# Stage one of a long convolution: the last 128 columns of four tiles in one eviction of 1024, with two staging buffers and a new order

## The chip, the cores and the metric

The kernel runs on one core of one Trainium2 chip. The metric is the device time of one execution in microseconds (us); lower is better. The engines are TensorE (PE in the profile), VectorE (DVE), ScalarE (ACT), GpSimd (POOL) and SyncE (SP), which issues nearly all DMA transfers.

## The reference

There are 2048 tokens of 640 channels. Two branches start from the same normalised input and are multiplied at the end.

```python
xn = _layernorm(A_q)
# branch A: short filter, then a convolution as long as the sequence, per channel
k_shift = sum_t k_pad[:, t:t+S, :] * shift_k[:, ks-1-t]      # ks = 4 taps
kv = k_shift * v
y  = irfft(rfft(kv padded to 2S) * rfft(ssm_k padded to 2S))[:S]   # causal convolution
s  = xn * (y + kv * ssm_D)
# branch B: a feed-forward block, 640 -> 1728 -> 640
g  = silu(gelu(xn @ w1 + b1) @ w2 + b2)
out = A_q + s * g
```

## The kernel before

**The convolution by matmuls.** The long convolution is a transform over time in two factors, a product by channel, and the way back. `K` stands for the filter `ssm_k`, `U` for the data `kv`; each is 16 tiles of 128 partitions by 640 channels. Stage one (`K1_i`, `U1_i`, L340) multiplies the two halves of 64 partitions of tile `i` by a matrix of sines `W`. Each half gives 640 columns. The first 512 go into one half of a PSUM buffer of two banks (`ps`), so one tile's two halves fill a buffer, and one eviction of 1024 columns (`Ke_i`, `Ue_i`, L175) copies it as bf16 into a staging buffer `st`. The other 128 columns are the remainder: `K1r_r`, `U1r_r` (L351) do it for a pair of tiles, four matmuls into half of a two-bank buffer, and `Ker_r`, `Uer_r` copy those 512 columns to the same staging buffer. Then `Ks_r`, `Us_r` (L358) store the staging buffer, four rows of 640 by 128 partitions, to a scratch in HBM (`scrK`, `scrU`). There are four staging buffers and three two-bank PSUM buffers.

Stage two loads the scratches back in another order (`KL`, L516, `UL`, L517), multiplies by small matrices (`K2`, `U2` L528, remainder `X2` L542), and evicts in place (`Kf`, `Uf`, `Xf`). The products by channel (`pm`, `pq`, L557, DVE) use the staging buffers again, stage three (`j1`, `j1r`, L563) and its evictions (`je`, `jer`) follow, `cs` (L613) and `cl` (L622) go through a third scratch `scrC`, and `i2` (L630) is the last step back; `ym` and `ad` (L634, L638) combine it with branch B.

**Branch B.** `bn`, `rs`, `xn` (L372, L385, L391) are the layer norm of a tile, `xt` (L401) and `xe` its transpose and the copy out. `f1` (L421) with `ge` (Gelu on ACT, L427) is the first product; tokens go in four chunks of four tiles. Chunk 0 goes through `f1` in halves of 256 tokens, two groups of hidden units to a bank; the other chunks take 512 tokens at once. `f2` (L457) with `si` (Silu, L461) and `gx` (L463) is the second product, a tile in two halves. `f1`, `f2` and `xt` share two PSUM buffers of a single bank (`psf`).

**Other work at the front.** `warm` (L656) is eleven matmuls on zeros ahead of everything, the `dm` operations (L663) are further dummies, `wq`, `wr`, `ws` make the matrix `W` in three pieces, `wm` and `we` (L320) spread the four short-filter taps over the partitions ("wx" in the text below), and `kv` (L485 to L494) is the short filter times `v`, in five groups on DVE, whose last operation (`kv_4`, L494) frees the U tiles of the group.

**What sets the order.** Each operation is declared with what it reads, writes and holds. The string `ORDER` lists all of them; the program is emitted in that order, and each engine and DMA queue runs its own operations in that order, waiting on semaphores. A suffix `/A` or `/D` says which of ACT and DVE makes an eviction. A buffer of a pool is taken at its first user in `ORDER` and is free again after its last.

```python
TB = (0, 4, 8, NT)     # W pieces by tile
NWARM = 11
IDLE = ((3, 1), (5, 1), (10, 1), (5, 0))     # dummies: how many, into which psf bank
```

Of the kernel before, what the change touches and what calls it, by code (L numbers as in the profile page):

```python
# [99 lines left out]
def h3_block(ctx: ExitStack, tc: tile.TileContext, x_d, k_d, v_d, sk_d, K_d, D_d, w1_d, b1_d, w2_d, out_d):  # L100
# [228 lines left out]
    def stage1(src, src_b, scr_, sb_, nm):  # L329
        for r in range(NG):  # L330
            o = Buf(pool=st)
            ob = [Buf() for _ in range(3)]
            pair = (2 * r, 2 * r + 1)
            for i in pair:
                pb = Buf(pool=ps)

                def s1(e, i=i, pb=pb):
                    for h in range(2):
                        hs = slice(64 * h, 64 * h + 64)
                        nc.tensor.matmul(out=pb.v[:, h, :], lhsT=W_t[hs, i, :], rhs=src[i][hs, 0:512], start=True, stop=True)  # L340

                op("%s1_%d" % (nm, i), "PE", s1, reads=[src_b[i], Wb[piece(TB, i)]], writes=[pb], hold=[o])
                op("%se_%d" % (nm, i), "ACT|DVE", lambda e, i=i, pb=pb, o=o: evict(
                    e, o.v[:, 2 * (i % 2):2 * (i % 2) + 2, 0:512], pb.v), reads=[pb], writes=[ob[i % 2]], hold=[o])
# [327 lines left out]
ORDER = """
c0 xl0 xl1 grid skl zz warm fix one1 wq1 Dl b1l Kl4 xl2 xl3 wq0 wr1 wr0 ws1 K1_6 bn1 wq2 ws0 Ke_6/A wm0 id we0/A bn0
K1r_3 dm0 K1_7 dm1 Ker_3/A b1c wr2 bn5 one0 Kl1 wm1 wm2 dm2 Ke_7/A ws2 rs0 xn1 xt1 xe1/A xn0 xt0 bn7 K1_5 dm3 xe0/A
bn4 bn6 we1/D Ke_5/A w1l2 w1l1 w1l0 f1_0_0_6 ge_0_0_7 Kl3 kl0 f1_0_0_4 K1_4 w1l3 Ks_3 ge_0_0_6 K1r_2 we2/A f1_0_0_2
ge_0_0_5 rs2 bn2 bn3 rs1 Kl2 ge_0_0_4 Ker_2/D f1_0_0_0 xn6 xn5 Ke_4/A ge_0_0_3 ge_0_0_2 K1r_6 ge_0_0_1 ge_0_0_0 xn7
xn4 K1_14 xt6 xe6/D K1_12 Ker_6/A xt7 xe7/D xn3 kv0_0 kv0_1m kv0_1a Ke_12/A xn2 xt5 kv0_2m kv0_2a kv0_3m kv0_3a kl1
vl0 kv0_4 kv1_0 xt4 K1r_7 xe5/A xe4/A K1_13 xt3 f1_1_0_4 xe3/A f1_1_0_7 kv1_1m kv1_1a Ke_13/A ge_1_0_4 Ker_7/A
ge_1_0_7 kv1_2m kv1_2a f1_1_0_11 Ke_14/A f1_1_0_1 ge_1_0_11 Ks_2 K1_15 K1_8 K1r_4 ge_1_0_1 xt2 Ker_4/A Kl0 xe2/A
Ke_15/A f1_1_0_0 f1_1_0_9 ge_1_0_0 ge_1_0_9 K1_9 f1_0_0_10 Ke_8/A f1_1_0_2 ge_0_0_10 Ks_7 ge_0_0_11 f1_0_2_12 K1_11  # L680
K1r_5 Ke_9/A Da ge_1_0_2 K1_10 ge_0_2_12 f1h_0 Ke_11/A geh_0 Ks_4 f1_1_0_12 Ke_10/A f1_1_0_6 ge_1_0_12 K1_2 kl2 K1_3
f1_1_0_8 vl1 Ker_5/A ge_1_0_6 Ke_3/A f1h_1 Ks_5 K1r_0 Ks_6 w2l1 K1_1 ge_1_0_8 geh_1 f1_1_0_3 w2l0 Ke_1/A ge_1_0_3
Ker_0/A f1_0_1_0 ge_0_1_1 kv1_3m kv1_3a kv1_4 xl5 ge_0_1_0 f1_1_0_10 f1_1_0_5 Ke_2/A ge_1_0_10 U1_1 U1r_0 ge_1_0_5
K1r_1 kv2_0 f1_0_1_6 f1_0_0_8 Uer_0/A Ue_1/A ge_0_1_7 ge_0_1_6 kv2_1m U1_0 U1r_2 kv2_1a ge_0_0_9 ge_0_0_8 Uer_2/A
f1_0_1_2 Ker_1/A ge_0_1_3 ge_0_1_2 kv2_2m Ks_1 sm0 kv2_2a sm1 Ue_0/A f1_0_1_4 vl2 ge_0_1_5 ge_0_1_4 kv2_3m f1_0_1_10
K1_0 ge_0_1_11 bn12 U1_4 U1_5 ge_0_1_10 bn15 Ue_5/A Ue_4/A f1_0_1_8 Us_2 kl3 ge_0_1_9 ge_0_1_8 f2_7_1 si_7_1 gx_7_1
bn13 ss f2_0_1 Ke_0/A si_0_1 gx_0_1 bn14 Ks_0 f2_3_1 si_3_1 kv2_3a U1r_3 Us_0 Uer_3/A U1_6 U1_7 Ue_7/A f2_6_0 Ue_6/A
gx_3_1 U1r_1 kv2_4 U1_3 si_6_0 U1_2 f2_5_0 sx f2_1_1 Uer_1/A kv3_1m Ue_3/A rs4 kv3_0 Ue_2/A vl3 U1_11 U1r_5 si_5_0
xn15 gx_5_0 kv3_1a xn14 kv3_2m gx_6_0 xn12 kv3_2a U1_10 kv3_3m xt14 si_1_1 gx_1_1 Ue_11/A xe14/A Ue_10/A Uer_5/A
f2_4_1 xt12 kv3_3a si_4_1 U1r_4 gx_4_1 U1_8 U1_9 f2_6_1 xe12/A Ue_9/A Uer_4/A si_6_1 Ue_8/A f2_2_0 Us_3 kv3_4 kv4_1m  # L690
kv4_0 xl4 gx_6_1 si_2_0 kv4_1a xt15 xe15/A Us_5 U1_12 U1_13 KL2 bn11 U1r_6 Uer_6/A kv4_2m bn9 kv4_2a kv4_3m Ue_12/A
# [63 lines left out]
```

## Time and profile before

| what | value |
|---|---|
| runs of the kernel | 185.24, 185.7, 188.32 us; median 185.7 |
| the profiled execution: its own time | 185.44 us |
| the profiled execution: span, first to last instruction | 183.4 us |
| PE busy | 176.8 us, 96% |
| DVE busy | 157.8 us, 86% |
| ACT busy | 142.3 us, 78% |
| DMA | 50.32 MB, mean 274 GB/s |
| granted PE clock | 1.00 |

Shares are of the span. A row of a timeline has the start, the duration, engine, line, operation, output and input, and in square brackets the idle time of the engine before it with what ended it. Rows that follow each other can overlap by a little, as the engines start the next instruction before the last has drained, so the distance between starts is the cost of one in a row. The ends of matmuls are modelled. `SPq` is the DMA queue of SP; a DMA's landing is counted from its issue.

### The profile page before, as it was taken

What the parts mean: (1) busy time and instruction counts of PE and PEld (TensorE: products, weight loads), DVE (VectorE), ACT (ScalarE), POOL (GpSimd) and SP (SyncE); (2) the same over time, 40 slices, a digit from 0 to 9 for tenths busy, and PEclk for the clock granted to TensorE, in tenths of its full rate; (3) what the DMA queues carried; (4) which work ended last, traced back from release to release, by engine and by line L of the source; (5) the groups of instructions that cost most, each with busy time, mean ns of one, the idle gap of its engine ahead of it and who ended that gap; (6) DMA issues with size and microseconds to landing.
All of it is one profiled execution on the core that took longest, in us unless ns stands there. A gap on an engine that the chain in (4) does not pass through costs nothing.

```text
span 183.4 us, 5038 instructions
## 1 busy us (share of the span) xinstructions
PE 176.8 (96%) x2111; PEld 103.0 (56%) x2111; DVE 157.8 (86%) x261; ACT 142.3 (78%) x217; POOL 16.4 (9%) x32
## 2 busy tenths in 40 slices
PE   7998899999999999999999999999999999999992
PEld 2366545444877566666653343434334688898781
DVE  7799699999999999997589997999999631599992
ACT  5699999999999969867689989999989831641021
POOL 4404003600001520002000000000000000000000
PEclk9999999999999999999999999999999999999999
DMA  5999996599987995997999497880161857998183
GB/s 133 405 396 289 396 423 270 164 376 405 390 291 270 332 358 193 346 383 276 307 389 391 127 265 241 274 274 15 45 244 54 331 194 240 358 377 276 45 313 116
DMA packets 24503, 50.32 MB, mean 274 GB/s; under 512 B 3807, under 2 KB 18465, under 8 KB 24226
## 3 DMA queue, kind: packets, MB, share of 16 engines
q1 hardware_dynamic: 24334, 50.01, 76.4%
q8 instruction: 16, 0.26, 0.6%
q10 hardware_dynamic: 148, 0.01, 0.1%
q14 instruction: 5, 0.04, 0.1%
HBM read 31.14 MB, written 18.35 MB: 270 GB/s over the span
## 4 chain that ended last, share of the span: by engine, by line
PE 89%; ACT 8%; DVE 1%; issue 1%; ACTq 0%; DVEq 0%
PE psf L457 34%; PE psf L421 30%; PE ps L563 6%; PE ps L528 4%; PE ps L340 4%; PE psf L656 3%; ACT st L175 3%; PE ps L630 2%; PE psf L401 2%; PE ps L542 1%; ACT hT L427 1%; ACT xnT L175 1%; PE psf L435 1%; PE ps L351 1%; ACT W L233 1%; ACT L427 1%
## 5 line engine op out<-in xcount | busy, mean ns | idle before, releaser
L457 PE MATMUL psf<-w,hT 128*64 128x320 bf16 (+6 forms) x672 | 64.5, 299 | 0.0
L421 PE MATMUL psf<-xnT,w 128*128 128x512 bf16 (+1 forms) x320 | 62.7, 340 | 1.4 <-ACT hT L427 1.2
L457 PEld LDWEIGHTS <-hT 128*64 128x64 bf16 (+3 forms) x672 | 46.9, 106 | 15.3 <-issue 2.9
L421 PEld LDWEIGHTS <-w 128*128 128x128 bf16 x320 | 28.9, 97 | 29.9 <-issue 11.5
L175 ACT CAST ku<-ps 128x1024 bf16<-128x1024 f32 (+1 forms) x43 | 39.5, 950 | 2.2 <-PE ps L563 1.1
L175 ACT CAST st<-ps 128x1024 bf16<-128x1024 f32 (+1 forms) x46 | 39.4, 898 | 1.6 <-PE ps L340 1.6
L427 ACT ACTIVATE hT<-psf,b1f 128x512 bf16<-128x512 f32 (+1 forms) x64 | 37.3, 633 | 1.1 <-PE psf L421 0.5
L461 ACT ACTIVATE sl<-psf 128x320 bf16<-128x320 f32 (+2 forms) x32 | 14.1, 440 | 30.6 <-PE psf L457 29.6
L175 DVE CAST ku<-ps 128x1024 bf16<-128x1024 f32 (+1 forms) x24 | 27.9, 1174 | 4.9 <-PE ps L528 2.3
L557 DVE TENSOR_TENSOR st<-ku 128x2048 bf16<-128x2048 bf16 (+1 forms) x32 | 24.7, 818 | 0.1
L463 DVE TENSOR_TENSOR xn<-xn,sl 128x320 bf16<-128x320 bf16 (+2 forms) x32 | 10.0, 316 | 10.0 <-ACT sl L461 9.9
L492 DVE TENSOR_TENSOR ku<-ku 128x2560 bf16<-128x2560 bf16 (+1 forms) x15 | 18.2, 1215 | 0.3
L489 DVE TENSOR_TENSOR ku<-ku 128x2560 bf16<-128x2560 bf16 (+1 forms) x15 | 18.3, 1217 | 0.2
L372 DVE BATCH_NORM_STATS2 stats<-x 128x6 f32<-128x320 bf16 x32 | 13.9, 475 | 0.9 <-DMA x<-in_x 0.9
L634 DVE TENSOR_TENSOR xn<-ps,xn 128x640 bf16<-128x640 f32 x16 | 12.7, 816 | 1.6 <-PE ps L630 1.6
L563 PE MATMUL ps<-st,I 32*64 32x512 bf16 (+1 forms) x384 | 11.1, 344 | 0.0
L528 PE MATMUL ps<-ku,F 64*32 64x512 bf16 x256 | 9.9, 379 | 0.0
L563 PEld LDWEIGHTS <-I 32*64 32x64 bf16 x384 | 4.9, 104 | 6.0 <-issue 4.1
L494 DVE TENSOR_TENSOR ku<-ku 128x2560 bf16<-128x2560 bf16 (+1 forms) x5 | 7.1, 1426 | 0.1
L401 PE MATMUL psf<-ident,xn 128*128 128x128 bf16 x80 | 6.9, 219 | 0.3 <-DVE xnT L175 0.3
L401 PEld LDWEIGHTS <-xn 128*128 128x128 bf16 x80 | 5.1, 97 | 3.2 <-issue 2.4
L391 DVE TENSOR_SCALAR xn<-x,mv,rstd 128x640 bf16<-128x640 bf16 x16 | 6.5, 437 | 0.0
(72 smaller groups left out, 125.3 us busy)
## 6 DMA issues: line engine op xcount, KB each, us to landing
scrK<-st SPq DMA_DIRECT2D x8, 640.0 KB, 4.8
scrU<-st SPq DMA_DIRECT2D x8, 640.0 KB, 6.0
ku<-scrK SPq DMA_DIRECT2D x8, 640.0 KB, 5.4
ku<-scrU SPq DMA_DIRECT2D x8, 640.0 KB, 6.6
scrC<-ku SPq DMA_DIRECT2D x8, 640.0 KB, 4.2
ku<-scrC SPq DMA_DIRECT2D x8, 640.0 KB, 5.5
ku<-in_v SPq DMA_DIRECT2D x4, 640.0 KB, 10.2
out<-x SPq DMA_DIRECT2D x15, 160.0 KB, 1.9
```

What stands on the lines that cost most here:

```text
L175: (nc.scalar.copy if e == "ACT" else nc.vector.tensor_copy)(out=out_, in_=in_)
L372: nc.vector.bn_stats(out=stats[:, i, h, :], in_=x_t[:, i, h * H:(h + 1) * H])
L401: nc.tensor.transpose(out=o[:, t, :], in_=xn_t[:, i, t * P:(t + 1) * P], identity=ident[:])
L421: nc.tensor.matmul(out=pb.v[:, u * n:u * n + n], lhsT=w1_t[:, ft, t, :], rhs=xnTb[c].v[:, a // P:(a + n) // P, t, :], start=(t == 0), stop ...
L427: op("ge_%d_%d_%d" % (c, r, ft), "ACT", lambda e, c=c, ft=ft, u=u, a=a, n=n, pb=pb: nc.scalar.activation(out=hTb[c].v[:, ft, a:a + n], in_ ...
L457: nc.tensor.matmul(out=pb.v[m:n, 0:hw], lhsT=hTb[c].v[0:M, ft, q * P + m:q * P + n], rhs=w2_t[0:M, ft, hs], start=(ft == 0), stop=(ft == F ...
L461: op("si_%d_%d" % (i, h), "ACT", lambda e, pb=pb, s_=s_, hw=hw: nc.scalar.activation(out=s_.v[:, 0:hw], in_=pb.v[:, 0:hw], func=ACT.Silu), ...
L489: op("kv%d_%dm" % (r, j), "DVE", lambda e, i=i, n=n, j=j, t=t, wb=wb: nc.vector.tensor_tensor(out=t.v[:, 0:n, :], in0=k_t[:, i + 3 - j:i + ...
L492: op("kv%d_%da" % (r, j), "DVE", lambda e, n=n, t=t, a=a: nc.vector.tensor_tensor(out=a.v[:, 0:n, :], in0=a.v[:, 0:n, :], in1=t.v[:, 0:n, ...
L528: nc.tensor.matmul(out=pb[ri].v[32 * j:32 * j + 32, a, :], lhsT=F2_t[64 * a:64 * a + 64, ri, :], rhs=B.v[64 * a:64 * a + 64, j, 0:512], st ...
L557: nc.vector.tensor_tensor(out=o, in0=u, in1=k, op=ALU.mult)
L563: nc.tensor.matmul(out=pb[j // 2].v[64 * a:64 * a + 64, j % 2, 0:n], lhsT=I1_t[32 * j:32 * j + 32, t, :], rhs=rhs(slice(32 * j, 32 * j + 3 ...
```

## The change

- The remainder of stage one is done for four tiles at a time: eight matmuls fill both banks of a PSUM buffer, and one eviction copies 1024 columns to two staging buffers, two tiles' remainders to each. So K and U have four remainder groups each instead of eight.
- The four staging buffers become parts of one tile `st`, so that one instruction can address two of them, whichever two and in whichever order.
- A staging buffer is stored when its two tiles and the shared remainder are evicted. A group of four tiles holds two staging buffers from its first matmul on.
- The order is new throughout, with the choice of ACT or DVE for each eviction, and the dummies are 10, 6 and 5 instead of 3, 5, 10 and 5. All merged evictions are on ACT.

```diff
-    st_t = [sb.tile([P, 4, D], BF16, name="st%d" % i)[:] for i in range(4)]
+    st_a = sb.tile([P, 16, D], BF16, name="st")
+    st_t = [st_a[:, 4 * i:4 * i + 4, :] for i in range(4)]
...
     def stage1(src, src_b, scr_, sb_, nm):
-        for r in range(NG):
-            o = Buf(pool=st)
-            ob = [Buf() for _ in range(3)]
-            pair = (2 * r, 2 * r + 1)
-            for i in pair:
-                pb = Buf(pool=ps)
+        for g in range(NG // 2):
+            o = [Buf(pool=st) for _ in range(2)]
+            ob = [[Buf() for _ in range(2)] for _ in range(2)]
+            rest = Buf()
+            quad = range(4 * g, 4 * g + 4)
+            for i in quad:
+                pb, oi = Buf(pool=ps), o[i % 4 // 2]
...
-            def s1r(e, pair=pair, pb=pb):
-                for i in pair:
+            def first(o):
+                return 0 if o[0].v.offset < o[1].v.offset else 1
+
+            def s1r(e, quad=quad, pb=pb, o=o, first=first):
+                for i in quad:
+                    n = P * (i % 4 ^ 2 * first(o))
                     for h in range(2):
                         hs = slice(64 * h, 64 * h + 64)
-                        nc.tensor.matmul(out=pb.v[:, h, P * (i % 2):P * (i % 2) + P], lhsT=W_t[hs, i, :], rhs=src[i][hs, 512:D],
+                        nc.tensor.matmul(out=pb.v[:, h, n:n + P], lhsT=W_t[hs, i, :], rhs=src[i][hs, 512:D],
                                          start=True, stop=True)
...
-            op("%ser_%d" % (nm, r), "ACT|DVE", lambda e, pb=pb, o=o: evict(
-                e, o.v[:, :, 512:D].rearrange("p (i h) c -> p h i c", h=2),
-                pb.v[:, :, 0:2 * P].rearrange("p h (i c) -> p h i c", i=2)), reads=[pb], writes=[ob[2]], hold=[o])
-            op("%ss_%d" % (nm, r), "SP", lambda e, r=r, o=o: nc.sync.dma_start(
-                out=by_q(scr_)[:, 4 * r:4 * r + 4, :], in_=o.v), reads=ob + [o], writes=[sb_[r]])
+            def er(e, pb=pb, o=o, first=first):
+                d0, d1 = (o[first(o) ^ k].v[:, :, 512:D] for k in range(2))
+                dst = bass.AP(tensor=d0.tensor, offset=d0.offset, ap=[d0.ap[0], [d1.offset - d0.offset, 2], [2 * D, 2], [D, 2], [1, P]])
+                evict(e, dst, pb.v.rearrange("p h (r i c) -> p r i h c", r=2, i=2))
...
+            for r in range(2):
+                op("%ss_%d" % (nm, 2 * g + r), "SP", lambda e, g=g, r=r, o=o: nc.sync.dma_start(
+                    out=by_q(scr_)[:, 8 * g + 4 * r:8 * g + 4 * r + 4, :], in_=o[r].v), reads=ob[r] + [rest, o[r]], writes=[sb_[2 * g + r]])
...
-IDLE = ((3, 1), (5, 1), (10, 1), (5, 0))
+IDLE = ((10, 1), (6, 1), (5, 0))
```

The two orders, PE's part only, up to the first `f2` and around the last U tiles:

```
before: warm K1_6 wm0 K1r_3 dm0 K1_7 dm1 wm1 wm2 dm2 xt1 xt0 K1_5 dm3 f1_0_0_6 f1_0_0_4 K1_4 K1r_2 f1_0_0_2 f1_0_0_0
        K1r_6 K1_14 xt6 K1_12 xt7 xt5 xt4 K1r_7 K1_13 xt3 f1_1_0_4 f1_1_0_7 ... U1_1 U1r_0 K1r_1 ... U1_0 U1r_2 ... U1_4 U1_5 f1_0_1_8 f2_7_1
        ... K2_2 f2_3_0 f2_2_1 U1_14 U1r_7 U1_15 f2_0_0
after:  warm K1_6 wm2 wm0 dm0 wm1 dm1 xt0 xt1 dm2 f1_0_0_6 f1_0_0_4 K1_7 K1r_1 K1_5 f1_0_0_0 f1_0_0_2
        K1_14 K1_4 xt4 xt7 K1_12 xt5 xt6 K1r_3 xt2 K1_15 f1_1_0_6 f1_1_0_1 ... f1_0_1_8 f2_7_1
        ... U1r_2 U1_10 f2_5_1 f2_6_1 U1_11 U1_12 U1_13 xt14 f2_2_1 K2_2 f2_2_0 U1_15 U1r_3 U1_14 xt15 f2_3_0
```

ACT's part up to the first 512-column `f1` of chunk 1:

```
before: ws1 ws0 Ke_6 we0 Ker_3 Ke_7 ws2 xe1 xe0 Ke_5 ge_0_0_7 ge_0_0_6 we2 ge_0_0_5 ge_0_0_4 Ke_4 ge_0_0_3 ge_0_0_2
        ge_0_0_1 ge_0_0_0 Ker_6 Ke_12 xe5 xe4
after:  ws1 ws2 we0 Ke_6 we1 xe0 xe1 ws0 ge_0_0_6 ge_0_0_7 ge_0_0_4 ge_0_0_5 Ker_1 Ke_5 ge_0_0_1 ge_0_0_0 ge_0_0_3
        ge_0_0_2 Ke_4 xe7 Ke_12 xe6
```

The loads and stores on SP are reordered with the rest: the first U store comes later, ahead of it all eight K stores, and the store of the U tiles 8 and 9 stands behind two loads of stage two.

More of the change, by code (lines that the diff above doesn't have):

```diff
@@ L340, in s1 @@
                         nc.tensor.matmul(out=pb.v[:, h, :], lhsT=W_t[hs, i, :], rhs=src[i][hs, 0:512], start=True, stop=True)
[L342 to L344 removed]
+                op("%s1_%d" % (nm, i), "PE", s1, reads=[src_b[i], Wb[piece(TB, i)]], writes=[pb], hold=[oi])
@@ L345, in stage1 @@
+                op("%se_%d" % (nm, i), "ACT|DVE", lambda e, i=i, pb=pb, oi=oi: evict(
+                    e, oi.v[:, 2 * (i % 2):2 * (i % 2) + 2, 0:512], pb.v), reads=[pb], writes=[ob[i % 4 // 2][i % 2]], hold=[oi])
             pb = Buf(pool=ps)
-            def s1r(e, pair=pair, pb=pb):
-                for i in pair:
+            def first(o):
[3 more added lines that the diff above has]
+                    n = P * (i % 4 ^ 2 * first(o))
@@ new lines, in stage1 @@
+            op("%s1r_%d" % (nm, g), "PE", s1r, reads=[src_b[i] for i in quad] + [Wb[w] for w in sorted({piece(TB, i) for i in quad})], writes=[pb], hold=o)
+            op("%ser_%d" % (nm, g), "ACT|DVE", er, reads=[pb], writes=[rest], hold=o)
+            for r in range(2):
+                op("%ss_%d" % (nm, 2 * g + r), "SP", lambda e, g=g, r=r, o=o: nc.sync.dma_start(
+                    out=by_q(scr_)[:, 8 * g + 4 * r:8 * g + 4 * r + 4, :], in_=o[r].v), reads=ob[r] + [rest, o[r]], writes=[sb_[2 * g + r]])
@@ L670 @@
 NWARM = 11
-IDLE = ((3, 1), (5, 1), (10, 1), (5, 0))
+IDLE = ((10, 1), (6, 1), (5, 0))
 ORDER = """
[L673 to L681, printed above, removed]
@@ L716 @@
+os_15_0 f2_15_1 si_15_1 gx_15_1 ad_15_1 os_15_1
 """
```

76 lines of the change are left out of this document (41 added, 35 removed).

## The prediction

> **What bounds the kernel now.** I read the page first, then the busy times of the engines in stretches, and then the timelines of the stretches where TensorE (PE) is not full.
>
> ```profile
> span 183.4 us, 5038 instructions
> ...
> PE 176.8 (96%) x2111; PEld 103.0 (56%) x2111; DVE 157.8 (86%) x261; ACT 142.3 (78%) x217; POOL 16.4 (9%) x32
> ...
> 0.00:6.08 6.08, 4.88 (x13) 1.56 (x13) 4.99 (x17) 3.14 (x5) 2.22 (x13) 1.00 0.63 196
> 6.08:22.34 16.26, 14.72 (x133) 9.48 (x134) 13.59 (x35) 15.19 (x25) 4.12 (x7) 1.00 0.99 368
> 22.34:43.15 20.81, 20.36 (x133) 9.72 (x133) 20.50 (x15) 20.69 (x33) 4.32 (x8) 1.00 0.83 320
> 43.15:157.80 114.65, 114.65 (x1510) 63.95 (x1511) 97.15 (x151) 95.41 (x142) 5.72 (x5) 1.00 0.76 266
> 157.80:180.00 22.20, 22.17 (x327) 18.33 (x322) 21.02 (x44) 7.52 (x13) 0.00 (x0) 1.00 0.74 261
> 180.00:183.40 3.40, 0.00 (x0) 0.00 (x0) 0.55 (x2) 0.36 (x1) 0.00 (x0) 1.00 0.20 65
> ```
>
> After the length, the columns of a stretch are busy us of PE, PEld, DVE, ACT, POOL, then the granted clock and DMA. From 43.15 to 157.80 us PE is busy for all of 114.65 us, and to 180.00 it misses 0.03. ACT, which the change relieves, is full only before that: 15.19 of 16.26 and 20.69 of 20.81 us. So an eviction saved after 43 us buys nothing by itself. The time changes only if PE reaches a given amount of work sooner in the first 43 us, or if the new order puts a hole into the full 137 us.
>
> **The change part by part: the eviction.** Sixteen evictions of 512 columns (eight each for K and U) become eight of 1024. The columns of a timeline row are start and duration; the cost of one in a row of work is the distance to the next start.
>
> ```profile
> 37.87 0.58 ACT L175 CAST st<-ps 128x512 bf16<-128x512 f32 x1
> 38.34 0.70 ACT L427 ACTIVATE hT<-psf,b1f 128x512 bf16<-128x512 f32 x1
> 38.92 1.02 ACT L175 CAST st<-ps 128x1024 bf16<-128x1024 f32 x1
> 39.81 0.72 ACT L427 ACTIVATE hT<-psf,b1f 128x512 bf16<-128x512 f32 x1
> ...
> L461 ACT ACTIVATE sl<-psf 128x320 bf16<-128x320 f32 x30 | 13.2, 440 | 27.1 <-PE psf L457 26.1 <-ACT ku L175 0.9
> ```
>
> A 512 costs 0.47 us (37.87 to 38.34), a 1024 costs 0.89 (38.92 to 39.81). Two against one is 0.94 against 0.89: 0.05 us saved, 0.4 us over eight. The trace has no eviction into two buffers in runs of 128; the bounds are 0.89, the nearest row of this size, and 0.94 if the runs cost as much as the two pieces did. I take 0.89, as the 512s went through runs of 128 already. Neither end matters to the time: in the U half ACT waits 26.1 us for PE (L461 row), and the K half is counted below. The matmuls stay the same, four times four becoming two times eight, so PE gains nothing, and two dummy matmuls fewer fall into the front's sum.
>
> **The order at the front.** The rest is the rewritten order. Its first half-conversion (f1, L421) comes before most of the K tiles now.
>
> ```profile
> 6.01 0.61 PE L340 MATMUL ps<-x,W 64*128 64x512 bf16 x2
> 6.55 0.72 PE L320 MATMUL ps<-hT,ones 1*128 1x512 bf16 x2
> ...
> 8.83 0.82 PE L320 MATMUL ps<-hT,ones 1*128 1x512 bf16 x3
> 9.58 1.26 PE L663 MATMUL psf<-hT 128*128 128x256 bf16 x10
> 10.68 0.72 PE L401 MATMUL psf<-ident,xn 128*128 128x128 bf16 x10
> 11.34 0.39 PE L340 MATMUL ps<-x,W 64*128 64x512 bf16 x2
> ...
> 12.65 2.34 PE L421 MATMUL psf<-xnT,w 128*128 128x256 bf16 x20
> ...
> 22.34 4.48 PE L421 MATMUL psf<-xnT,w 128*128 128x512 bf16 x20 [0.16 <-ACT xnT L175]
> ...
> 40.59 2.33 PE L421 MATMUL psf<-xnT,w 128*128 128x512 bf16 x15 [0.20 <-ACT hT L427]
> 43.15 2.46 PE L421 MATMUL psf<-xnT,w 128*128 128x512 bf16 x10 [0.23 <-ACT hT L427]
> ...
> 52.49 0.59 PE L340 MATMUL ps<-ku,W 64*128 64x512 bf16 x4
> ...
> 54.12 5.88 PE L457 MATMUL psf<-w,hT 128*128 128x320 bf16 x42
> ...
> 11.31 1.29 ACT L175 COPY xnT<-psf 128x640 bf16<-128x640 bf16 x2
> 12.46 1.06 ACT L175 CAST st<-ps 128x1024 bf16<-128x1024 f32 x1
> 13.99 1.28 ACT L427 ACT_TABLE_LOAD   x1 [0.47 <-PE psf L421]
> 15.28 0.84 ACT L427 ACTIVATE hT<-psf,b1f 128x256 bf16<-128x256 f32 x2
> 16.01 0.59 ACT L175 CAST ku<-ps 128x512 bf16<-128x512 f32 x1
> ...
> 3.54 2.76 SPq L288 DMA_DIRECT2D w<-in_w x3
> ...
> w<-in_w SPq DMA_DIRECT2D x1, 640.0 KB, 7.2
> ```
>
> After the warm-up PE now runs: one K tile 0.54 (6.01 to 6.55), three L320 matmuls 0.75 (8.83 to 9.58), ten dummies 1.10 (9.58 to 10.68), two L320 matmuls 0.50, six dummies 0.66, two transposed tiles 0.66 (10.68 to 11.34). From 6.01 that is 10.22. ACT follows: wx eviction from 7.30 to 8.19, K eviction to 9.08, wx eviction to 9.97, two xnT copies of 0.575 (11.31 to 12.46 for two) to 11.12. So f1 starts at about 11.2 instead of 12.65. Its weights are the seventh load on SP in both orders; they land at 3.54 + 7.2 = 10.7, in time.
>
> From there to the first 512-column f1 (22.34 before) both orders put the same work through PE, seven K tiles, four L351 groups' worth, seven transposed tiles and four f1 pairs, and ACT sets the pace. Before, ACT has eight Gelus of 0.365 (15.28 to 16.01 for two), two 1024s, two 512s and two copies after 15.28: 2.92 + 1.78 + 0.94 + 1.15 = 6.79, ending at 22.07. The trace has 22.34, so 0.27 are waits. After, the table load comes 1.34 after f1's start (12.65 to 13.99), at 12.54; Gelus start 1.29 later, at 13.83. The list has four 1024s: 2.92 + 3.56 + 1.15 = 7.63, with the same 0.27 of waits ends at 21.73. A lead of 1.45 us at f1 has shrunk to 0.6. A K eviction that stood ahead of the table load (Ke_5) and a remainder of 1024 in place of one of 512 (with a wx eviction the other way) cost 0.84 there.
>
> From 22 us to the first f2, ACT's list is lighter: four U tiles and two U remainders, which it used to evict before the first Silu, come later, so fourteen 1024s and seven 512s (15.8 us) become fourteen 1024s (12.5). PE then sets the pace, and of its two waits for Gelu (0.20 and 0.23) I let a quarter vanish. The lead is 0.7 us (0.6 and 0.1), bounds 0 and 1.45 + 0.43 = 1.9.
>
> **The order behind, and the waits it adds.** Each store of U (and K) now waits for the matmuls of four tiles, and the four hold two of four staging buffers. PE's last U tiles wait for the last kv product on DVE.
>
> ```profile
> 78.43 3.98 PE L457 MATMUL psf<-w,hT 128*128 128x320 bf16 x28
> 82.35 0.39 PE L340 MATMUL ps<-ku,W 64*128 64x512 bf16 x2
> ...
> 79.97 0.88 DVE L372 BATCH_NORM_STATS2 stats<-x 128x6 f32<-128x320 bf16 x2
> 80.88 0.21 DVE L373 BATCH_NORM_AGGREGATE mv<-stats 128x2 f32<-128x12 f32 x1
> 81.01 0.77 DVE L494 TENSOR_TENSOR ku<-ku 128x1280 bf16<-128x1280 bf16 x1
> 81.70 0.32 DVE L463 TENSOR_TENSOR xn<-xn,sl 128x320 bf16<-128x320 bf16 x1
> ...
> DMA to landing us min/median/max: 3.4/4.8/7.0
> ```
>
> That product is done at 81.70 and PE takes it at 82.35, 0.65 to spare. In the new order DVE has two statistics of 1.04 (79.97 to 81.01) and one L463 of about 0.3 less before it, 2.4 us; PE has one f2 half of 1.96 (3.92 for two, 78.43 to 82.35) and one transposed tile of 0.33 less, 2.3. DVE's chain starts behind PE's transposes, so both engines lead by about 0.7 and the 0.65 stays: no wait, price zero. If that cover goes, PE stands still for what is missing, and behind it nothing else can start.
>
> The last U quad needs the buffer of the tiles 8 and 9. Their merged eviction is the third behind its matmuls on ACT (0.89 + 0.58 + 0.89, so 2.4 us), and PE has four f2 halves (7.84), five U tiles of 0.3 (0.59 for two at 52.49) and a transposed tile before the next merged group, 9.7 us, and the matmuls of one K2 on top. That leaves about 7.5 us for the store, and the stores took 3.4 to 7.0 us between 55 and 100 us (the last row above). No wait, with 0.5 to spare at the worst. The waiting eviction would hold up the whole of ACT: two tile evictions, the Silus that free PE's two banks, then the last two stores and all eight U loads behind them on SP.
>
> Later, K and U evictions are dealt between ACT and DVE nearly as before, the six f2 halves that cover the way through scrC stay six, and the chain after the last matmul (3.40 us) is the same. I cost these at zero; the cover is the 114.65 us in which PE never waited.
>
> **The sum.** The profiled execution took 185.44 us, its span and 2.04 around it. 185.44 - 0.7 = 184.7 us. The median of the runs shown is 185.7, 0.26 above that execution.
>
> **The rivals.** *The lead is eaten by 43 us.* For it: ACT is 99% full there (20.69 of 20.81), there are only two single banks for f1, and a 1024 in place of a 512 makes the gap between two Gelus 0.42 longer. Against: the list is 3.3 us shorter. PE's waits grow by 0.7: 185.4 us, no change.
>
> *The staging buffers bind (slower than before).* Place: the merged eviction of the last U quad, at about 80 us. It decides once the store of tiles 8 and 9 needs over 7.5 us; at 10.5, half as long again as the longest, ACT stands for 3.0 us, and PE, with two banks to fill, for nearly as much: 184.7 + 3.0 = 187.7 us. Against: all stores of that stretch landed within 7.0.
>
> *PE's clock.* Between 17 and 21.7 us the new order leaves PE short K tiles and transposes with waits for ACT between them. In the first 5 us the eleven warm-up matmuls took 4.88 us, 0.444 each, against 4.48 / 20 = 0.224 at 22.34. If PE fell back to that rate for as long as the warm-up lasted, it would lose 4.88 / 2, 2.4 us: 187.1. Against: the granted clock is 1.00 in every stretch, and PE stays busy more than half of the time. The Trainium skill ("TensorE: Matmul & The Clock Gate", Part 1) has the clock halved after an idle window of some 3.4 us, and Part 4 says that transposes do not count as busy in the same way. By that rule the stretch could just trip it; in the trace the matmuls at 22.34, behind transposes and K tiles as well, run at 0.224.
>
> *The whole lead stays.* If the 1.45 at f1 holds and both Gelu waits go: 185.44 - 1.9 = 183.5.
>
> **How the numbers follow.** Forecast 0.45, lead eaten 0.22, staging 0.12, whole lead 0.10, clock 0.08, anything worse 0.03. The range runs from a little under the whole lead, 183.3, to the staging case, 187.7. The bound of 2%, about what a measurement of this kernel can tell from no change, is 3.7 us: under 182.0 nothing here reaches (0.03), over 189.4 only two of the bad cases together or an unseen hole (0.07).
>
> **What would show it.** In the profile after: the eight merged evictions at 0.89 to 0.94 us from start to start; the first L421 at 11.2 (not 12.65), the first 512-column one at 21.7, the first L457 near 52 (54.12 less 1.2 for the four U tiles that moved behind it, their remainders and the lead); PE full from there to the end; the last L494 before the U tile that needs it. I am wrong if PE waits for ACT more than 2 us between 22 and 52, if it shows any wait near 80 or 93 us, or if matmuls of 512 columns take over 0.4 us apart after 17 us.

## The result and the profile after

The changed kernel takes 184.53 us in the median (184.39 to 185.18), against 185.70 for the kernel before: a ratio of 0.996, interval 0.9943 to 0.9978. By the 2% bound that is no change, and by the interval a gain of some 0.7 us. The later rounds agree: there the kernel before took 185.20 to 185.29 us (medians of 9 to 29 runs). Forecast was 184.7. The profiled execution took 184.39, its span 182.6 us.

The page's head, and the busy times in the same stretches as before:

```profile
span 182.6 us, 5023 instructions
...
PE 175.6 (96%) x2109; PEld 104.0 (57%) x2109; DVE 157.8 (86%) x258; ACT 143.9 (79%) x212; POOL 16.4 (9%) x32
...
6.08:22.34 16.26, 14.57 (x134) 9.53 (x134) 15.55 (x38) 14.97 (x25) 5.39 (x13) 1.00 0.94 336
22.34:43.15 20.81, 20.72 (x133) 9.72 (x132) 20.38 (x33) 20.05 (x31) 4.87 (x3) 1.00 1.00 370
43.15:157.80 114.65, 114.65 (x1530) 64.50 (x1529) 96.05 (x131) 98.53 (x143) 2.80 (x3) 1.00 0.76 267
157.80:180.00 22.20, 21.25 (x310) 18.61 (x306) 20.63 (x46) 6.94 (x13) 0.00 (x0) 1.00 0.67 231
```

PE is again busy for all of 114.65 us in the middle, and the granted clock is 1.00 throughout. Between 22.34 and 43.15 ACT has come down from 20.69 to 20.05 us and PE has gone up from 20.36 to 20.72. In the last stretch PE shows less only because it is done sooner.

Where the time went is read from PE's timeline, at six places that every kernel here passes:

```profile
6.02 0.39 PE L342 MATMUL ps<-x,W 64*128 64x512 bf16 x2 [0.46 <-DMA x<-in_ssm_k]
...
11.30 2.41 PE L431 MATMUL psf<-xnT,w 128*128 128x256 bf16 x20
...
21.84 4.48 PE L431 MATMUL psf<-xnT,w 128*128 128x512 bf16 x20
...
51.49 3.97 PE L467 MATMUL psf<-w,hT 128*128 128x320 bf16 x28
...
93.85 1.24 PE L431 MATMUL psf<-xnT,w 128*128 128x512 bf16 x5
...
156.64 0.71 PE L640 MATMUL ps<-ku,G 128*64 128x512 bf16 x8
```

These are the first K tile, the first f1, the first f1 of 512 columns, the first f2, the first f1 of the third and fourth chunk, and the first i2 product. The differences of their starts give a table that all later readings use. The four U tiles and two U remainders that stood ahead of the first f2 in the kernel before are taken out of its third stage and put into the fourth, to compare like with like:

```profile
45.54 0.39 PE L340 MATMUL ps<-ku,W 64*128 64x512 bf16 x2
45.77 0.28 PE L351 MATMUL ps<-ku,W 64*128 64x128 bf16 x4
45.88 0.28 PE L351 MATMUL ps<-x,W 64*128 64x128 bf16 x4
...
48.38 0.39 PE L340 MATMUL ps<-ku,W 64*128 64x512 bf16 x2
48.60 0.28 PE L351 MATMUL ps<-ku,W 64*128 64x128 bf16 x4
48.81 3.52 PE L421 MATMUL psf<-xnT,w 128*128 128x256 bf16 x30
...
52.49 0.59 PE L340 MATMUL ps<-ku,W 64*128 64x512 bf16 x4
53.01 1.26 PE L421 MATMUL psf<-xnT,w 128*128 128x256 bf16 x10
```

From start to next start they take 0.34 + 0.43 + 0.52 = 1.29 us.

| us | before | after | lead gained | predicted |
|---|---|---|---|---|
| first K tile to first f1 | 6.64 | 5.28 | 1.36 | 1.45 |
| to first 512-column f1 | 9.69 | 10.54 | -0.85 | -0.84 |
| to first f2 (U work taken out) | 30.49 | 29.65 | 0.84 | 0.1 |
| to first f1 of chunks 3 and 4 (U work in) | 42.06 | 42.36 | -0.30 | 0 |
| to first i2 | 62.75 | 62.79 | -0.04 | 0 |
| to the end of the span | 25.76 | 25.96 | -0.20 | 0 |

The sum is 0.81, and the spans differ by 0.8. The forecast of 0.7 was right in sum, with one stage mis-sized by 0.7 and three losses of 0.54 missed; that the two nearly cancel is luck. The first row is also the least certain. It compares one execution of each kernel, and in the profiles below the same front took 6.42 us twice in the order of before, and 5.28 to 5.75 in the new one. So the lead made there is 0.7 to 1.4 us, and the 0.81 fits the spans of these two executions alone.

Ratios and intervals here and below leave out executions in a slower state (of the kernel before, the one at 188.32 us) and so are not quotients of the medians, and two profiles below, of fifteen dummies and of the last w1 piece early, were taken in that state (granted clock 0.79 between 6 and 22 us), so that only their stages that begin behind 25 us are read.

### The profile page after: what moved, and what is told of

Its sections match the earlier page's. It is cut to its first block, busy times and chain, and to the rows that moved or that the text cites. A ratio compares the mean times of both kernels' runs of the same rounds, so it can differ in the third digit from the quotient of the medians.

```text
span 182.6 us, 5023 instructions
## 1 busy us (share of the span) xinstructions
PE 175.6 (96%) x2109; PEld 104.0 (57%) x2109; DVE 157.8 (86%) x258; ACT 143.9 (79%) x212; POOL 16.4 (9%) x32
## 3 DMA queue, kind: packets, MB, share of 16 engines
HBM read 31.14 MB, written 18.35 MB: 271 GB/s over the span
## 4 chain that ended last, share of the span: by engine, by line
PE 72%; DVE 11%; ACT 11%; DMA 2%; issue 2%; SPq 0%; ACTq 0%
PE psf L431 27%; PE psf L467 25%; DVE xn L644 6%; PE ps L573 6%; PE ps L538 5%; ACT st L176 4%; PE ps L342 4%; ACT hT L437 3%; DVE x L648 3%; DMA x<-in_ssm_k 2%; PE psf L411 2%; DVE xn L473 1%; PE ps L552 1%; DVE x L656 1%; ACT ku L176 1%
## 5 line engine op out<-in xcount | busy, mean ns | idle before, releaser
L431 PE MATMUL psf<-xnT,w 128*128 128x512 bf16 (+1 forms) x320 | 61.9, 340 | 0.1
L467 PEld LDWEIGHTS <-hT 128*64 128x64 bf16 (+3 forms) x672 | 47.5, 106 | 14.8 <-issue 3.2
L176 ACT CAST st<-ps 128x1024 bf16<-128x1024 f32 x39 | 39.3, 1028 | 0.3 <-PE ps L342 0.2
L176 DVE CAST ku<-ps 128x1024 bf16<-128x1024 f32 (+1 forms) x25 | 28.7, 1153 | 4.8 <-PE ps L573 2.6
L567 DVE TENSOR_TENSOR st<-ku 128x512 bf16<-128x512 bf16 (+1 forms) x32 | 25.0, 815 | 0.6 <-PE ps L573 0.5
L499 DVE TENSOR_TENSOR ku<-ku 128x2560 bf16<-128x2560 bf16 (+1 forms) x15 | 19.1, 1275 | 0.2
L502 DVE TENSOR_TENSOR ku<-ku 128x2560 bf16<-128x2560 bf16 (+1 forms) x15 | 18.2, 1214 | 0.2
L573 PE MATMUL ps<-st,I 32*64 32x512 bf16 (+1 forms) x384 | 11.2, 344 | 0.0
L176 ACT COPY xnT<-psf 128x640 bf16<-128x640 bf16 x12 | 8.4, 724 | 0.0
L401 DVE TENSOR_SCALAR xn<-x,mv,rstd 128x640 bf16<-128x640 bf16 x16 | 7.5, 492 | 0.1
```

The costliest lines, as they stand in the source:

```text
L176: (nc.scalar.copy if e == "ACT" else nc.vector.tensor_copy)(out=out_, in_=in_)
L431: nc.tensor.matmul(out=pb.v[:, u * n:u * n + n], lhsT=w1_t[:, ft, t, :], rhs=xnTb[c].v[:, a // P:(a + n) // P, t, :], start=(t == 0), stop ...
L467: nc.tensor.matmul(out=pb.v[m:n, 0:hw], lhsT=hTb[c].v[0:M, ft, q * P + m:q * P + n], rhs=w2_t[0:M, ft, hs], start=(ft == 0), stop=(ft == F ...
L499: op("kv%d_%dm" % (r, j), "DVE", lambda e, i=i, n=n, j=j, t=t, wb=wb: nc.vector.tensor_tensor(out=t.v[:, 0:n, :], in0=k_t[:, i + 3 - j:i + ...
L502: op("kv%d_%da" % (r, j), "DVE", lambda e, n=n, t=t, a=a: nc.vector.tensor_tensor(out=a.v[:, 0:n, :], in0=a.v[:, 0:n, :], in1=t.v[:, 0:n, ...
L567: nc.vector.tensor_tensor(out=o, in0=u, in1=k, op=ALU.mult)
```

## The experiments

Ratios are against the kernel before on the same chip, with 95% intervals. The cuts from an order show the part of the engines that the text names.

### Two evictions instead of the merged one

```diff
-            op("%ser_%d" % (nm, g), "ACT|DVE", er, reads=[pb], writes=[rest], hold=o)
+            for k in range(2):
+                op("%ser_%d_%d" % (nm, g, k), "ACT|DVE", lambda e, k=k, er=er: er(e, k), reads=[pb], writes=[rests[k]], hold=o)
```

> The changed kernel with one thing taken back: each 1024-column remainder is evicted by two instructions of 512 columns, one behind the other on the same engine, instead of one. Matmuls, banks and order stay. Theory (the rewritten order carries the gain, the merged eviction is worth nothing): ScalarE does 8 x 0.05 = 0.4 us more, four of them before 52 us, and the time stays within 0.3 us of the changed kernel, 184.4 to 184.8 us. Rival (the merged eviction carries it): the gain of about 1 us goes, 185.4 to 185.7 us.

Measured: 184.71 us, 0.9972 (0.9959 to 0.9985), within the 184.4 to 184.8 of the theory. With the kernel before at 185.22 us in this round, the rival's loss of the whole gain would be a ratio of 1, which the interval leaves out. So the order carries at least most of the gain; the difference of 0.2 us to the changed kernel lies inside both intervals, and the times cannot say that it is nothing. In this profile the third stage is 0.47 longer than in the changed kernel (30.12), nearly all of it in one wait. It looks as if the split cost that, until one sees the same unit in a kernel whose evictions are merged (the one with the y sums first, below):

```profile
27.32 0.74 PE L446 MATMUL psf<-xnT,w 128*64 128x256 bf16 x10 [0.43 <-ACT hT L438]
```

```profile
27.27 0.74 PE L445 MATMUL psf<-xnT,w 128*64 128x256 bf16 x10 [0.37 <-DMA w<-in_w]
```

The first row is of the split kernel, the second of the merged one. The unit is the first 64-row half of f1, and it waits for the last piece of w1. In the changed kernel the load of that piece is issued at 18.25 and took 8.4 us (first row, and the last row of the view of that tile's DMA), so it landed at 26.65, and the unit started at 26.68. In the split kernel the same load, issued at 17.52, took 9.8 us and landed at 27.3, which is when the unit started there, though the wait names a Gelu:

```profile
18.25 0.52 SPq L289 DMA_DIRECT2D w<-in_w  x1
...
DMA to landing us min/median/max: 8.4/8.4/8.4
...
26.68 0.74 PE L445 MATMUL psf<-xnT,w 128*64 128x256 bf16 x10
```

That wait comes and goes from one execution to the next with the load, whatever the evictions are. After the first f2 the split kernel needs 42.33 us to the next mark, the merged ones 42.32 to 42.36: there the saved 0.05 us per eviction buys nothing, as predicted.

### The order of before from 93 us, and from 147 us

Both orders have done the same set of operations at the first X2 (93 us) and again at 147 us, so they can be joined there.

```diff
 # e2_front_new
-ORDER = new order
+ORDER = new order up to xt8 (93 us) + order of before from f1_3_0_0 on
 # e4_tail_old
-ORDER = new order
+ORDER = new order up to gx_11_0 (147 us) + order of before from cl_5 on
```

> The changed kernel's code, with its order up to the first X2 (about 93 us, where both orders have done the same operations) and the order of before from there. Theory (the lead is made before 93 us and the new order behind loses a little of it): the first chunk-3 f1 starts at 93.8 to 93.9 us as in the changed kernel, 1.04 us ahead of before, and all of it reaches the end, 184.2 to 184.4 us. Rival (the order behind 93 us adds to the gain): 184.8 to 185.5 us.

> The changed kernel's code, with its order up to about 147 us and the order of before for the tail (f2, i2 and the outputs of the last two chunks). Theory (the new tail order loses 0.2 us of the lead, since the last i2 products wait for VectorE): last Silu at about 179.0 us and 184.2 to 184.4 us. Rival (the tails are worth the same): 184.4 to 184.7 us, the time of the changed kernel. Second rival (the old tail was fitted to the old middle): over 184.8 us.

Measured: 184.17 us, 0.9949 (0.993 to 0.9967), with the rest old, and 183.96 us, 0.9938 (0.9919 to 0.9958), with the tail alone old. Both stages behind the cut say why: 62.75 and 62.79 us to the first i2 (the middles are worth the same), and 25.71 and 25.65 us from there to the end, against 25.96 in the changed kernel. So the gain is made before 93 us, and by the profiles the new tail gives back 0.25 to 0.3 of it; the intervals of the three times overlap. The first chunk-3 f1 came at 94.24 in the first of the two, not at 93.8 to 93.9 as expected: that execution needed 5.75 us from the first K tile to the first f1, where the changed kernel's profile shows 5.28. This front stage varies from 5.28 to 5.75 over seven profiles in which its code is the same or nearly so, and the end moves with it.

### The y sums first

```diff
-ad_10 gx_8_0 ym_9 ym_0 ym_8
+ad_10 ym_9 ym_0 gx_8_0 ym_8
```

> The changed kernel with one VectorE instruction moved in the tail: the Silu product of tile 8 (second half) goes behind the y sums of tiles 9 and 0 instead of ahead of them. Theory (the tail's loss of 0.2 to 0.3 us is this: VectorE stands 0.49 us for a Silu with finished i2 banks behind it, so the second i2 after it waits 0.27 us): the eight i2 matmuls that took 0.81 us at 162.63 take 0.54, first i2 to the end of the last f2 22.24 us instead of 22.51, and the time 0.2 to 0.3 us below the changed kernel, 184.1 to 184.3 us. Rival (the wait comes from elsewhere in the tail, VectorE being nearly full there): 22.5 us and no change.

Measured: 184.49 us, 0.9952 (0.9932 to 0.9973). The rows of the changed kernel, then of this one:

```profile
162.63 1.01 PE L640 MATMUL ps<-ku,G 128*64 128x512 bf16 x8
163.44 2.10 PE L467 MATMUL psf<-w,hT 128*64 128x320 bf16 x28
...
161.33 0.33 DVE L473 TENSOR_TENSOR xn<-xn,sl 128x320 bf16<-128x320 bf16 x1 [0.49 <-ACT sl L471]
161.57 3.74 DVE L644 TENSOR_TENSOR xn<-ps,xn 128x640 bf16<-128x640 f32 x5
```

```profile
163.31 0.71 PE L640 MATMUL ps<-ku,G 128*64 128x512 bf16 x8
163.86 2.07 PE L467 MATMUL psf<-w,hT 128*64 128x320 bf16 x28
```

The eight i2 matmuls took 0.81 us and take 0.55 now, and the tail 25.67 instead of 25.96. In the profile the theory holds: VectorE stood 0.49 us for a Silu, with finished i2 banks behind it, and PE paid for it a little later, in a wait too short for a bracket of its own. The time does not show it: 184.49 is outside the 184.1 to 184.3 of the theory, by the ratios it came down by about 0.15 us, and that is inside the intervals. The span of this profile, 183.0, also holds the w1 wait of 0.37.

### Fifteen and ten dummies instead of five

```diff
-IDLE = ((10, 1), (6, 1), (5, 0))
+IDLE = ((10, 1), (6, 1), (15, 0))   # and (10, 0) in the second kernel
```

> The changed kernel with ten more dummy matmuls (fifteen instead of five) just ahead of the first f1, which adds 1.1 us to TensorE there and computes nothing else. Theory of the prediction (ScalarE sets the pace between the first f1 and 22 us, and it starts when f1 does, so the early f1 counts in full): first f1 at 12.4 us, first 512-column f1 at about 22.9, and 185.4 to 185.7 us, the whole gain gone. Rival (the early f1 is worth little, because the lead is made between 22 and 52 us by the lighter list of ScalarE): first 512-column f1 below 22.3 us, and 184.4 to 184.8 us.

> The changed kernel with five more dummy matmuls (ten instead of five) just ahead of the first f1, half of the earlier step. Theory (the early f1 counts one for one): first f1 and first 512-column f1 0.45 to 0.55 us later relative to the first K tile than in the changed kernel, and the time 0.4 to 0.6 us longer, half-way between the changed kernel and the one with fifteen, about 185.0 us. Rival (what the front gives is fixed by data that arrive later, and only fifteen dummies cross that point): no change, 184.4 to 184.6 us.

Measured: 185.53 us, 1.0022 (1.0005 to 1.0038), with fifteen, and 184.99 us, 0.9984 (0.9967 to 1.0002), with ten. With the changed kernel at 0.996 that is 1.15 and 0.44 us for 1.1 and 0.55 us of dummies. The first is clear of both intervals, the second is not. With ten, first f1 stands 5.78 us behind the first K tile, which five dummies reached once too (5.75), and the next three stages are 10.54, 29.63 and 42.32: nothing there absorbs the delay. But these two profiles have one wait that no other profile here has behind 96 us, for a load of the third scratch in the tail. The row is of the kernel with ten dummies; with fifteen the same wait is 0.73 us:

```profile
166.66 0.73 PE L640 MATMUL ps<-ku,G 128*64 128x512 bf16 x8 [0.45 <-DMA ku<-scrC]
```

Their tails take 26.57 and 26.88 us in place of 25.96, so 0.6 and 0.9 more. So the medians fit an early f1 that counts one for one, but the profiles do not separate it from this load, and whether the dummies make the load late is not shown.

### The U work later in the kernel before

```diff
-f1_1_0_5 U1_1 U1r_0 K1r_1 ... U1_0 U1r_2 f1_0_1_2 ... K1_0 U1_4 U1_5 f1_0_1_8 f2_7_1 si_7_1 f2_0_1 si_0_1 f2_3_1 si_3_1
+f1_1_0_5 K1r_1 ... f1_0_1_2 ... K1_0 f1_0_1_8 f2_7_1 si_7_1 U1_1 U1r_0 f2_0_1 si_0_1 U1_0 U1_4 U1r_2 f2_3_1 si_3_1 U1_5
```

> The kernel before (single remainders, its own order) with one move: the four U tiles, the two U remainders and the store that stand before the first f2 go behind the first three f2 halves, with their evictions behind the first Silus, as the changed order has it. Theory (between 22 and 52 us TensorE was late for Gelu, because ScalarE also had these evictions; without them its waits go): first f2 at 54.12 - 1.29 (the moved TensorE work) - 0.6 to 0.85 = 52.0 to 52.2 us, waits for Gelu before it under 0.1 us, and the time 0.5 to 0.9 us below before. Rival (those waits come from the K tiles and the two single banks, the U evictions only fill ScalarE): first f2 at 52.6 to 52.9 us, and the time within 0.2 us of before.

Measured: 187.59 us, 1.0128 (1.0096 to 1.016). My theory fell. The third stage is 30.62, not shorter than the 30.49 of before without the U work, and the two waits for Gelu are where they were:

```profile
40.74 2.33 PE L421 MATMUL psf<-xnT,w 128*128 128x512 bf16 x15 [0.20 <-ACT hT L427]
43.30 2.46 PE L421 MATMUL psf<-xnT,w 128*128 128x512 bf16 x10 [0.23 <-ACT hT L427]
...
58.83 0.29 PE L351 MATMUL ps<-ku,W 64*128 64x128 bf16 x4 [0.67 <-ACT st L175]
...
62.72 0.39 PE L340 MATMUL ps<-ku,W 64*128 64x512 bf16 x2 [0.85 <-ACT st L175]
```

They stand ahead of the first U eviction (46.23 us in the kernel before), so taking those away cannot help. What the move did is in the last two rows: put between the first f2 halves in a bunch, the U evictions overrun ScalarE, and PE waits 1.52 us for banks; the stage takes 44.24 us instead of 42.06. The changed order spreads the same work and shows no such wait.

### One K tile and one K remainder later as well

```diff
-f1h_1 K1r_0 K1_1 f1_1_0_3 ... f1_0_1_6 f1_0_0_8
+f1h_1 f1_1_0_3 ... f1_0_1_6 K1r_0 K1_1 f1_0_0_8
```

> The kernel before with the U work moved behind the first f2 as in the run e7_u_later, and then one K tile and one K remainder (matmuls and evictions) moved from 40 us to the room at 46 to 50 us that this leaves. The stretch from the first 512-column f1 to the first f2 is what counts here, 30.62 us in e7_u_later, 29.65 in the changed kernel; the time itself carries the loss of e7_u_later behind 53 us and tells nothing. Theory (the 0.8 us gained there come from K evictions that no longer stand between Gelus bunched before 46 us; the U work only has to leave room for them): the waits of 0.20 and 0.23 us for Gelu go, and the stretch takes 29.9 to 30.2 us. Rival (the waits come from the order of the f1 units on their two banks): the stretch stays at 30.5 to 30.7 us with waits for Gelu of 0.3 us or more.

Measured: 187.96 us in a single run, and a third stage of 31.14 us, longer by 0.52 and outside both ranges:

```profile
40.36 4.50 PE L421 MATMUL psf<-xnT,w 128*128 128x512 bf16 x25 [0.65 <-ACT hT L427]
...
50.65 0.60 PE L421 MATMUL psf<-xnT,w 128*128 128x256 bf16 x4 [0.45 <-ACT hT L427]
```

The wait of 0.20 grew to 0.65, and the one of 0.23 behind it is gone. The first ends 18.24 us into the stage (40.36 less 22.12), as in the run before (40.74 less 22.49): the moved evictions stood behind the Gelu that it waits for, and the K tile was work that PE did while ScalarE freed one of the two single banks. The second was a wait for a Gelu behind the moved evictions. The rows are ScalarE's, in the kernel before and then in this one:

```profile
41.37 1.01 ACT L175 CAST st<-ps 128x1024 bf16<-128x1024 f32 x1
42.41 0.69 ACT L427 ACTIVATE hT<-psf,b1f 128x512 bf16<-128x512 f32 x1
```

```profile
41.64 0.69 ACT L427 ACTIVATE hT<-psf,b1f 128x512 bf16<-128x512 f32 x1 [0.51 <-PE psf L421]
```

Without the eviction ahead of it, this Gelu waits for PE. What lengthens the stage is the new wait of 0.45, behind the place to which the evictions were moved. So my theory held for one wait and the rival for the other: PE's waits go by which evictions stand just ahead of a Gelu on ScalarE, and by what PE has to do until it is done.

### The store that the last U quad waits for

```diff
 # e8_late_store
-U1_12 Us_4 U1_13 xt14 xe14 Us_2 ... KL3 gx_6_1 Us_5
+U1_12 U1_13 xt14 xe14 Us_2 ... KL3 gx_6_1 Us_5 Us_4
 # e8c_buffer_bound
+U1_12 U1_13 xt14 xe14 ... KL3 gx_6_1 Us_5 Us_4 Us_2
```

> The changed kernel with the store of U tiles 8 and 9 moved behind the store of tiles 10 and 11 on SyncE, about 3.2 us later (from 71.6 to about 75). Nothing else is moved. Theory (the staging buffers are what the last U quad waits for once that store is late; in the changed kernel it lands some 0.5 us before the merged eviction at 79.66): landing 7 to 8 us after issue, so ScalarE stands 2.5 to 3.5 us before the last merged U eviction, TensorE runs out of free banks about 1.5 us after that began and waits 1 to 3 us near 82 us, and the time is 185.5 to 187.5 us. Rival (a store issued later lands sooner, 5 us or less, because fewer transfers run beside it): no wait over 0.5 us and 184.4 to 184.8 us.

> The changed kernel with the stores of U tiles 8 and 9 and of tiles 4 and 5 both moved behind the store of tiles 10 and 11 on SyncE, so that the last U quad has to take the staging buffer of tiles 10 and 11 (buffers go out in the order in which their stores stand), whose store cannot be issued before about 74.9 us. Theory (the staging buffers bind): it lands 6.8 to 8.2 us after issue, 81.7 to 83.1 us, so ScalarE stands 1.7 to 3.1 us before the last merged U eviction (about 80.0 us); TensorE has free banks for about 0.7 us less than that and loses 1.0 to 2.4 us between 82 and 87 us; 185.5 to 187.0 us. Rival (the banks hide it, as they hid the late store in the run before): ScalarE stands, TensorE waits under 0.4 us, 184.4 to 185.0 us.

Measured: 184.98 us, 0.9981 (0.9955 to 1.0006), and 184.81 us, 0.9976 (0.996 to 0.9991). The first did not test what I meant: buffers go out in the order in which their stores stand, so the last tiles took the buffer of tiles 4 and 5, stored at 67.78, instead of waiting; its one new wait, 0.41 us, is K2's for a load of scrK. In the second they do take the late one, of tiles 10 and 11, and ScalarE still does not stand. The rows are the three late stores, the landing of the first of them, and the last merged eviction, with no idle time before it:

```profile
74.92 1.78 SPq L368 DMA_DIRECT2D scrU<-st  x3
...
DMA to landing us min/median/max: 3.4/3.4/3.4
...
79.31 0.53 ACT L471 ACTIVATE sl<-psf 128x320 bf16<-128x320 f32 x1
79.71 1.94 ACT L176 CAST st<-ps 128x1024 bf16<-128x1024 f32 x2
```

It landed at 78.3, after 3.4 us, where I had expected 6.8 to 8.2. The same store in the changed kernel, issued at nearly the same time but behind two others and a load issued at 72.46:

```profile
71.56 0.81 SPq L368 DMA_DIRECT2D scrU<-st  x2
...
DMA to landing us min/median/max: 7.6/7.6/7.6
...
74.80 8.65 SPq L368 DMA_DIRECT2D scrU<-st  x3
...
DMA to landing us min/median/max: 8.2/8.2/8.2
```

The landing lines are of the second store of the pair at 71.56, and of the first one of the three at 74.80. So the price of the rival, 3.0 us, was never seen: the buffers do not bind even with 4.8 us between store and eviction. Neither theory of mine was right; the store was faster than both assumed. The order of the stores is not all that counts: in the first of the two kernels no store had been issued for 7 us when it went out at 74.86 (the one before at 67.78), and it took 6.8 us.

### The first w1 piece first, and the last one early

```diff
 # e13_weights_first: e4_tail_old with
-xl2 w1l0 w1l2 w1l1        IDLE = ((10, 1), (6, 1), (5, 0))
+xl2 w1l2 w1l1 w1l0        IDLE = ((10, 1), (6, 1), (1, 0))
 # e15_last_w1_early: e4_tail_old with
-kl0 Ks_3 Kl2 w1l3
+kl0 w1l3 Ks_3 Kl2
```

> The changed kernel's code with its order up to 147 us and the old tail (as e4_tail_old), and two more edits at the front: of the three loads of w1 the piece that the first f1 reads is issued first (it was the second, at about 3.55 us, landing at about 11.2), and the five dummy matmuls just ahead of the first f1 become one. Theory (the early f1 counts one for one, and behind the dummies it is the weights that it waits for): weights landed by 10.7 us, first f1 at 10.7 to 10.9 instead of 11.3, and 0.3 to 0.6 us off e4_tail_old, 183.3 to 183.7 us. Rival (the pieces share the queues, so the first lands no earlier): first f1 at 11.0 to 11.3 and 183.9 to 184.1 us.

> The version with the old tail (e4_tail_old) and one more edit: the load of the last w1 piece (720 KB), which the 64-row f1 unit at 26.7 us reads, goes on SyncE from behind the first K store, where it is issued at 17.4 to 18.6 us, to ahead of it, right behind the first k load at about 12.3 us. Theory (TensorE's wait there, 0.37 us for this load in one profile, 0.15 in another, 0.43 in a third where a Gelu is named, is this landing at 26.7 to 27.3 us): landed by 24 us, that unit starts within 0.35 us of the K tile ahead of it, the stretch from the first 512-column f1 to the first f2 takes 29.5 to 29.6 us in place of 29.63 to 30.12, and the time is 0 to 0.3 us under e4_tail_old, 183.7 to 184.0 us where before takes 185.2. Rival (that load then takes bandwidth from the K tiles and k, which land later): a new wait of 0.3 us or more between 14 and 26 us, and 184.2 us or more.

Measured: 184.33 us, 0.9952 (0.9937 to 0.9968), and 184.36 us, 0.9941 (0.9927 to 0.9955). Neither beats the version with the old tail, 0.9938. In the first, f1 waits for its transposed input, which is as late as before:

```profile
11.27 2.34 PE L431 MATMUL psf<-xnT,w 128*128 128x256 bf16 x20 [0.33 <-ACT xnT L176]
```

In the second the 64-row unit follows its K tile after 0.32 us and no longer waits for w1, yet the third stage is 29.64, what it was in the profiles without that wait. So this edit takes away a wait of some executions and nothing from the others, and the median does not show it.

The lowest ratio is that of the changed kernel with the old tail, 183.96 us and 0.9938 of the kernel before; its interval overlaps with that of the changed kernel (0.9943 to 0.9978).

## Why the prediction was right, and where it was wrong

*PE is full behind 43 us, so an eviction saved there buys nothing.* Right: 114.65 of 114.65 us again, and splitting the evictions left the stage behind the first f2 as it was. (Read from start to start, two short waits of 0.14 and 0.07 us are hidden in the full rows of before, at 44.37 and 51.08.)

*The merged eviction takes 0.89, bounds 0.89 to 0.94.* Right. The rows are of the changed kernel:

```profile
79.66 1.93 ACT L176 CAST st<-ps 128x1024 bf16<-128x1024 f32 x2
81.47 0.71 ACT L176 COPY xnT<-psf 128x640 bf16<-128x640 bf16 x1
```

The merged one and the tile's behind it take 1.81 us from start to start, 0.905 each.

*First f1 at 11.2, first 512-column f1 at 21.73.* Measured 11.30 and 21.84. ScalarE's list, which took 0.84 us back of 1.45, was off by 0.01: the stage grew by 0.85. The profiles bear out that this stretch starts when f1 does: its length is 10.53 to 10.60 us in all nine profiles of the changed code whose clock stayed at 1.00, wherever f1 stood. That it runs at ScalarE's pace rests on the sum of ScalarE's list, which came out.

*From 22 us to the first f2 the lead grows by 0.1.* This is the term that was mis-sized: it grew by 0.84. I had let a quarter of PE's two waits for Gelu vanish, 0.1 of 0.43. All of both went: from 22.34 to 43.15 us PE misses 0.09 us (20.72 of 20.81), and missed 0.45 before. The other 0.4 the view of idle time could not tell me, since it sat inside rows counted as busy. One such row of before:

```profile
35.00 2.51 PE L421 MATMUL psf<-xnT,w 128*128 128x512 bf16 x10
```

These ten matmuls took 2.45 us (next start 37.45), and ten at 27.69 took 2.27 (next start 29.96). In the middle, at 36.28, two starts lie 0.40 us apart, where 0.22 is usual. Read in this way, from the starts of single matmuls in the trace, the stage before holds 1.15 us over the usual spacing of each kind, at seven places: 0.40, 0.27, 0.19 and 0.14 ahead of 43.15, 40.59, 36.28 and 44.37, and 0.16 at three others. The stage after holds 0.33, at two places: 0.22 ahead of 40.40 and, for the w1 piece, 0.11 ahead of 26.68. The difference, 0.82, is nearly all of the 0.84.

The reason that I gave, a lighter list of ScalarE, fits: between 22.34 and 54 us ScalarE never waits for PE before, and five times, 1.4 us in all, after. But it is not the U evictions that made it lighter where it counts. They stood behind the four large waits, and moving them alone left these waits as they were. What became lighter ahead of 44 us is the K work: up to the same twenty Gelus ScalarE makes nine evictions of 1024 and four of 512 columns before, ten of 1024 after, at 0.89 and 0.47 us 9.9 against 8.9. The run with one K tile later shows that moving K evictions takes away a wait behind them, and that the gain is lost again if they bunch elsewhere. Which exchanges of the new order did it I did not isolate.

*The stages behind lose nothing.* They lost 0.54. Of the 0.30 in the U stage, f2 takes 0.29 (31.52 us from start to start against 31.23 before): nine of its runs end in matmuls of 64 rows now, seven before. What such an end costs is shown by these rows of the changed kernel:

```profile
56.16 2.08 PE L467 MATMUL psf<-w,hT 128*128 128x320 bf16 x14
58.17 0.39 PE L342 MATMUL ps<-ku,W 64*128 64x512 bf16 x2
...
66.57 2.08 PE L467 MATMUL psf<-w,hT 128*128 128x320 bf16 x14
68.49 0.44 PE L411 MATMUL psf<-ident,xn 128*128 128x128 bf16 x5
```

An f2 half takes 2.01 us when a tile of 64 rows follows and 1.92 when a transpose of 128 rows does: 0.09 for the change, and 0.2 of the 0.29 for two more. The Trainium skill ("TensorEngine Tiling (Array Packing)", Key Properties) says that changing the tiling mode drains TensorE; the rows fit that and put 0.09 us on it. I had counted U tiles in quads as the same work; they are, but the number of runs that they cut f2 into is not. The 0.20 at the end is VectorE's order, shown above.

*The last kv product keeps 0.65 us to spare.* No wait, as said, but 0.35 is left:

```profile
77.92 0.82 DVE L504 TENSOR_TENSOR ku<-ku 128x1280 bf16<-128x1280 bf16 x1
78.66 0.32 DVE L473 TENSOR_TENSOR xn<-xn,sl 128x320 bf16<-128x320 bf16 x1
...
79.01 0.39 PE L342 MATMUL ps<-ku,W 64*128 64x512 bf16 x2
```

*The last quad's buffer comes free in time, with 0.5 us to spare at the worst.* Right: the store was issued at 71.56 and the eviction began at 79.66, 8.1 us later with no wait, and the store issued right behind it took 7.6. (The trace does not show the landing of the store itself.) But the bound under it was wrong: the U stores of the changed kernel took 4.0 to 9.4 us, not 3.4 to 7.0, so the step came out with some luck. The rival's condition, a store of over 7.5 us, also took the landing time for a property of the store. It depends on what else is under way: held back by 3 us, the store that the quad then needed was done in 3.4.

*The rivals.* The lead was not eaten by 43 us: PE waits 0.09 us there, not more than before. The clock stayed at 1.00 in the changed kernel's profile, and the first twenty f1 matmuls of 512 columns took 4.41 us (21.84 to 26.25), 0.22 each. A granted clock of half does occur, but elsewhere: the profiles of fifteen dummies and of the last w1 piece early show 0.50 between 10 and 14 us, and in both PE had waited for a load right behind the warm-up, 1.21 and 1.70 us, where it waited 1.00 or less in the others. That the wait is the cause is not shown. The whole lead (183.5) came close in a way: 2.2 us were gained at f1 and Gelu and 1.4 lost again in four stages.

## What to carry to other kernels

When a rewritten order moves the time little, cut the span at operations that every version passes and compare the stages: 0.8 us here was +2.2 and -1.4, and in the profile the tail's loss was handed back by joining the two orders. Where an engine is full, look for waits inside rows counted as busy: the same number of matmuls taking longer than elsewhere in the same trace. Before an experiment is read as taking load off an engine, look whether what it moved stood ahead of the wait or behind it. A wait that names one engine in one profile and a transfer in another belongs to whichever landed last there, so compare several executions before an edit is blamed for it.
